# Attention and routed experts on one core: new durations, hand-off times and priorities for the planner that writes the order of the attention stage

## The chip, the cores and the metric

One core of one Trainium2 chip runs the whole program. The metric is device time in microseconds, from the first to the last instruction of one execution, taken as the median of several executions. Lower is better.

## The reference

Two layers follow each other. The first is an attention layer over 8 batches of 8 heads, 1152 keys of 64 numbers, whose queries are averaged in pairs, so that 576 queries are left per head:

```python
q_pool = q.reshape(B, H, S // 2, 2, D).mean(axis=3)
scores = np.matmul(q_pool, k.transpose(0, 1, 3, 2)) / np.sqrt(D)
scores = scores - np.max(scores, axis=-1, keepdims=True)
attn = np.exp(scores)
attn = attn / (np.sum(attn, axis=-1, keepdims=True) + 1e-09)
x = np.matmul(attn, v)
```

The second layer takes the 4608 rows of 512 numbers that come out, gives each row to one of 8 experts of 576 places (greedily, by sorted gate logits), and computes `relu(x @ w1[e]) @ w2[e]` for the rows of each expert. Everything is float32.

## The kernel before

**Attention, pair by pair.** Two heads make a pair; there are 32 pairs, 0 to 31. A pair is handled in 18 steps (9 blocks of 128 keys for each of its two heads). A step has two halves of 288 queries, and each half is two matmuls into one of three PSUM banks `sc` (L466 and L467: the numbers are split into a high and a low part so that the product is exact enough), followed by an exponential on ScalarE (L470). One subtraction per step (L473, on GpSimd in most steps and on VectorE in the others) makes the low part `PM` of the exponentials. For two steps at a time 30 short matmuls (L483, 15 a step) multiply the exponentials with the values; this is called a block of `av` here.

**What a pair needs beforehand.** A bound on the scores of each query has to be known before the first exponential. For that the 27 `mm` matmuls of a pair (L401, into the three PSUM banks `ma`, `mb`, `mc`) compute a coarse product, and VectorE reduces each bank to a maximum (L405). When all 27 are reduced, L422 folds them, a PE transpose (L437) and a VectorE operation (L438) turn them into the tile `AU`, and two tiny transfers (L441) put `AU` into row 64 of `QB`, one of the operands of L467. So the first score matmul of a pair waits for this chain: last `mm`, its reduction, fold, transpose, `AU`, transfer. The `mm` matmuls of a pair run in the middle of the previous pair, and read `BD` (the queries laid out in blocks, L338, made of the averaged queries `QS`, L330, which come from the loaded tile `QD`) and `KH` (the high part of the keys, L347, made from the loaded tile `KD`).

**Transfers.** All of them are issued by SyncE, in one order, on one queue. A pair has loads `QD` (L317), two halves of `KD` (L321) and `VD` (L325), six copies per head inside SBUF that spread the high and low parts over the operands `KA`, `KB`, `QA`, `QB` (L357), the two tiny ones (L441), and every second pair a store (L584). `KA`, `KB`, `QA`, `QB` have two buffers, so the copies of a pair write over those of two pairs earlier, and must wait until the score matmuls of that head are through. An issue that waits holds back all that stand behind it on SyncE.

**The planner.** No order is written by hand. Every operation is added to a list by `Order.add`, with an engine, an assumed duration, the tiles that it reads and writes, and an extra delay `late` until others may use what it writes. `Order.emit` then plays all engines against each other in assumed time: each engine takes, of the operations that are ready, the one with the smallest priority, and the instructions are written in the order in which they were taken. The priority is the nominal place (in steps) plus `LEAD[tag]`; `LATE[tag]` is added to `late`; `WAIT[a][b]` is the assumed time of a hand-off from engine a to engine b and `OWN` the one to an operation of the same engine. A transfer is an operation of engine "SP" with a duration and a `late`. On the chip there is no planner: each engine runs its instructions in the written order, and waits for semaphores.

**Experts.** The second half of the program (`experts`, from about 890 us on) is planned by the same class with its own tables `EOWN`, `EWAIT`, `ELEAD`, `ELATE`.

Of the kernel before, what the change touches and what calls it, by code (L numbers as in the profile page):

```python
# [18 lines left out]
BF = mybir.dt.bfloat16  # L19
# [27 lines left out]
class Order:  # L47
# [3 lines left out]
    OWN = {"PE": 0, "ACT": 190, "DVE": 130, "POOL": 130, "SP": 60}  # L51
    WAIT = {"PE": {"ACT": 260, "DVE": 260, "POOL": 260, "SP": 260},
            "ACT": {"PE": 270, "DVE": 150, "POOL": 180, "SP": 150},
            "DVE": {"PE": 250, "ACT": 150, "POOL": 170, "SP": 150},
            "POOL": {"PE": 170, "ACT": 100, "DVE": 100, "SP": 100},
# [17 lines left out]
    def emit(self):  # L73
# [86 lines left out]
LEAD = {"av0a": 3.8, "av0b": -145.3, "av1a": -3.0, "expa": -95.5, "expb": 46.0, "mm": 1.0, "mc": -122.8, "mr": 77.4,  # L160
        "fold": 194.4, "kl": -40.7, "kh": 79.0, "ql": 264.0, "qs": 149.5, "vl": -310.1, "pmD": -154.7, "pmP": 95.3,
        "gl": -110.7, "x": -28.9, "aug": 20.5, "augt": -216.4, "vabs": -101.5, "store": 99.4, "bd": -11.1, "fill":
        -174.6, "qh": 62.0, "gc": -210.5, "vs": -182.4, "rc": -114.1, "gt": -29.9, "gm": -192.5, "vh": -23.5, "qka":
        3.2, "qkb": 0.4, "gp": -61.0, "gb": 146.7, "augd": 90.5}
LATE = {"mc": 200, "av1b": 0, "pmP": 150, "av0b": 0, "av1a": -350, "pmD": 300, "vh": -100, "av0a": 0, "expa": 50,
        "mm": -50, "mr": -100, "qka": -150, "expb": 50, "qkb": 50, "fold": 250, "aug": -100, "gt": -100, "gc": 0,
        "augt": 400, "gm": 100}
# [66 lines left out]
def attention(ctx, tc, top, kt, qt, v, wg, x_dram, L, npair=NPAIR):  # L234
# [81 lines left out]
    def load(n, t):  # L316
        od.add(t, "SP", 650, lambda: nc.sync.dma_start(QD[0], qt[n]), w=["QD"],  # L317
               late=4000 if not n else 6000 if n > 1 else 13000)
        for z in range(2):
            h = slice(z * M, z * M + M)  # L320
            od.add(t, "SP", 650, lambda h=h: nc.sync.dma_start(KD[0][:, h], kt[n][:, h]), w=[("KD", z)],  # L321
                   late=3000 + 1000 * z if not n else 5500 if n > 1 else 12000)

    def load_v(n, t):
        od.add(t, "SP", 650, lambda: nc.sync.dma_start(VD[0], v[n]), w=["VD"], late=6500)  # L325


    def split(n, t):
        i = n % 2
        od.add(t, "DVE", 650, lock=1, fn=lambda: nc.vector.tensor_tensor(QS[0], QD[0][:, 0], QD[0][:, 1], op=OP.add),  # L330
               r=["QD"], w=["QS"], tag="qs")
        od.add(t + 1, "ACT", 565, lambda: nc.scalar.copy(QH[i], QS[0]), r=["QS"], w=[("QH", i)], tag="qh")
# [7 lines left out]
        for s in range(2):  # L340
            if n:
                od.add(t + 1.1, "ACT", 575, bd(s, nc.scalar.copy), r=["QS"], w=[("BD", i, s)], tag="bd")
            else:
                od.add(t + 0.5, "DVE", 670, bd(s, nc.vector.tensor_copy), r=["QS"], w=[("BD", i, s)], tag="bd")
# [8 lines left out]
    def spread(n, t):  # L353
# [925 lines left out]
```

## Time and profile before

| | |
|---|---|
| median of 3 runs | 1394.06 us (1392.82 to 1394.68) |
| the profiled execution | 1397.87 us, of which the span from first to last instruction is 1396.0 us |
| busy, share of the span | PE 95%, weight loads 84%, VectorE 78%, GpSimd 57%, ScalarE 55% |
| granted TensorE clock | 0.980 of full speed, mean over the span |
| attention, first score matmul to the end | 23.9 to 892.6 us |

The profile numbers the engines' work by line of the kernel. PE is the matmul, PEld the weight load that goes with it, DVE is VectorE, ACT ScalarE, POOL GpSimd, SP SyncE, and a small q (SPq) means the engine's instruction sequencer. In a table of windows each engine has its busy time and, behind an x, the number of its instructions that ran in that window; the columns after the engines are the granted clock, the busy share of the DMA engines and the GB/s that they moved. Since each pair has 36 matmuls of L466, their number in a window tells how many pairs went by. In a list of waits, a row has who waited, for what, then the total, the number and the longest of these waits.

### The profile page before, as it was taken

To read this page: it belongs to the slowest core of one execution; us is meant where nothing else is said; L and a number is where in the kernel's file an instruction comes from. 1 tells how busy PE (TensorE), PEld (TensorE's weight loads), DVE (VectorE), ACT (ScalarE), POOL (GpSimd) and SP (SyncE) were. 2 spreads that over 40 slices of the span, in tenths; PEclk is the share of its full clock that TensorE was granted. 3 is DMA by queue.
4 is the path that set the end of the run, shared out by engine and by line. 5 is a ranking of instruction groups with operands and counts; after the bars stand their busy time and mean duration, and the time that the engine had idled before them with its cause. 6 is when DMAs were issued, how large, how long until landed. Compare 5 with 4: busy or idle time off the path is not lost.

```text
span 1396.0 us, 39631 instructions
## 1 busy us (share of the span) xinstructions
PE 1327.1 (95%) x15415; PEld 1179.3 (84%) x15415; DVE 1083.7 (78%) x2901; ACT 774.7 (55%) x1838; POOL 802.2 (57%) x739
## 2 busy tenths in 40 slices
PE   7899999999998998999999999779999999999996
PEld 6688999998887887998988998658888798898995
DVE  8888999898977889899999996588887678662220
ACT  5576777677665774777767766213424343343330
POOL 4375665655664463665655665335758585676731
PEclk9999999999998999999999999899999999999998
DMA  8866887776875766677767763031354353444400
GB/s 235 210 143 160 198 196 188 192 178 165 192 178 130 193 167 176 154 188 189 191 166 191 167 143 78 19 119 70 138 208 150 112 179 111 134 169 130 147 19 34
DMA packets 86840, 213.23 MB, mean 153 GB/s; under 512 B 12797, under 2 KB 37373, under 8 KB 84477
## 3 DMA queue, kind: packets, MB, share of 16 engines
q1 hardware_dynamic: 78172, 158.26, 46.3%
q0 software_dynamic: 8336, 52.44, 10.7%
q8 instruction: 121, 1.98, 0.6%
q14 instruction: 67, 0.54, 0.1%
q10 hardware_dynamic: 144, 0.02, 0.0%
HBM read 99.63 MB, written 18.87 MB: 85 GB/s over the span
## 4 chain that ended last, share of the span: by engine, by line
PE 78%; DVE 9%; DMA 4%; ACT 3%; issue 3%; SPq 1%; POOL 0%; POOLq 0%; ACTq 0%; DVEq 0%
PE av L483 15%; PE ph L1172 15%; PE po L1202 13%; PE sc L466 11%; PE sc L467 9%; PE ma L401 3%; PE mb L401 3%; PE mc L401 3%; DVE MX L405 3%; ACT P L470 1%; PE rt L845 1%; DVE PM L473 1%; DMA VD<-in_v_dram 1%; DMA QB<-AU 1%; PE po L1199 1%
## 5 line engine op out<-in xcount | busy, mean ns | idle before, releaser
L473 POOL TENSOR_TENSOR PM<-P 128x576 f16<-128x576 f32 x413 | 497.9, 1222 | 374.3 <-ACT P L470 318.3
L470 ACT ACTIVATE P<-sc 128x288 f32<-128x288 f32 x1152 | 420.2, 411 | 224.1 <-PE sc L467 204.8
L466 PE MATMUL sc<-QA,KA 128*128 128x288 f32 x1152 | 364.0, 326 | 11.7 <-ACT P L470 8.2
L467 PE MATMUL sc<-QB,KB 65*128 65x288 f32 (+1 forms) x1152 | 336.5, 301 | 5.4 <-DMA QB<-AU 3.0
L483 PE MATMUL av<-V,P 128*128 128x65 f16 (+1 forms) x5760 | 304.6, 193 | 0.0
L483 PE MATMUL av<-V,PM 128*128 128x65 f16 x2880 | 292.5, 195 | 0.7 <-POOL PM L473 0.7
L483 PEld LDWEIGHTS <-P 128*128 128x128 bf16 x5760 | 271.4, 98 | 24.0 <-issue 1.9
L483 PEld LDWEIGHTS <-PM 128*128 128x128 f16 x2880 | 265.4, 97 | 1.2 <-POOL PM L473 0.9
L466 PEld LDWEIGHTS sc<-QA,KA 128*128 128x128 f32 x1152 | 223.3, 194 | 29.6 <-ACT P L470 21.6
L467 PEld LDWEIGHTS sc<-QB,KB 65*128 65x128 f32 (+1 forms) x1152 | 223.2, 194 | 6.8 <-DMA QB<-AU 3.0
L405 DVE TENSOR_REDUCE MX<-mb 128x1 f32<-128x384 f32 x282 | 154.6, 548 | 24.4 <-PE mb L401 23.7
L405 DVE TENSOR_REDUCE MX<-ma 128x1 f32<-128x384 f32 x282 | 154.3, 547 | 22.5 <-PE ma L401 20.2
L1202 PE MATMUL po<-W2H,HX 128*128 128x512 f32 x512 | 167.4, 402 | 0.0
L405 DVE TENSOR_REDUCE MX<-mc 128x1 f32<-128x384 f32 x281 | 153.9, 548 | 8.1 <-PE mc L401 6.8
L1172 PE MATMUL ph<-XL,W1H 128*128 128x320 f32 (+1 forms) x512 | 152.4, 298 | 1.1 <-DVE XL L1071 1.1
L1172 PE MATMUL ph<-XH,W1H 128*128 128x320 f32 (+1 forms) x512 | 153.1, 299 | 0.0
L1172 PE MATMUL ph<-XH,W1L 128*128 128x320 f32 (+1 forms) x512 | 151.9, 297 | 0.0
L473 DVE TENSOR_TENSOR PM<-P 128x576 f16<-128x576 f32 x163 | 126.4, 796 | 19.4 <-ACT P L470 18.7
L1202 PE MATMUL po<-W2L,HX 128*128 128x512 f32 (+1 forms) x320 | 127.1, 397 | 0.0
L1177 ACT ACTIVATE HX<-ph 128x256 fp32r<-128x256 f32 (+1 forms) x128 | 52.3, 410 | 121.4 <-PE ph L1172 114.1
L401 PE MATMUL ma<-KH,BD 128*128 128x384 f32 x283 | 104.3, 369 | 8.9 <-ACT BD L338 4.6
L1181 DVE SCALAR_TENSOR_TENSOR HX<-ph,HX 128x256 fp32r<-128x256 f32 x128 | 53.4, 420 | 75.8 <-ACT HX L1177 75.6
(238 smaller groups left out, 2315.2 us busy)
## 6 DMA issues: line engine op xcount, KB each, us to landing
QD<-in_qt_dram SPq DMA_DIRECT2D x32, 576.0 KB
KD<-in_kt_dram SPq DMA_DIRECT2D x64, 288.0 KB
VD<-in_v_dram SPq DMA_DIRECT2D x32, 576.0 KB
KA<-KH SPq DMA_DIRECT2D x64, 288.0 KB
KB<-KH SPq DMA_DIRECT2D x64, 288.0 KB
KA<-KL SPq DMA_DIRECT2D x64, 288.0 KB
QA<-QH SPq DMA_DIRECT2D x128, 144.0 KB
QB<-QL SPq DMA_DIRECT2D x64, 144.0 KB
```

Source lines behind the costliest of these rows:

```text
L401: od.add(t, "PE", 180, lambda: nc.tensor.matmul(m[:, :384], BD[i][:, j, :], KH[i][:, 384 * c:384 * c + 384], start=True, stop=True), r=[(" ...
L405: od.add(t, "DVE", 466, lambda: nc.vector.tensor_reduce(MX[i][:, j, c:c + 1], m[:, :384], axis=AX.X, op=OP.max), r=[mk], w=[("MX", i, j, c ...
L466: nc.tensor.matmul(c[:, :288], KA[i][:, s, ks], QA[i][:, s, qs], start=True, stop=False)
L467: nc.tensor.matmul(c[:, :288], KB[i][:kr, s, ks], QB[i][:kr, s, qs], start=False, stop=True)
L470: od.add(g + 0.1 + 0.01 * t, "ACT", 291, lambda c=c, qs=qs: nc.scalar.activation(p[:, qs], c[:, :288], AF.Exp, scale=1.0 / 16), r=[ck], w= ...
L473: od.add(g + 0.2, en, dur, lock=1, fn=lambda: eng.tensor_tensor(pm, p, hi, op=OP.subtract), r=[("P32", g % NP, 0), ("P32", g % NP, 1)], w= ...
L483: nc.tensor.matmul(out, w[:, qs], v, start=kb == 0 and j == 0 and y == 0, stop=kb == NKB - 1 and y == 2, skip_group_check=True)
L845: nc.tensor.matmul(rb[:16 * nb, :8 * nb], GE[:, 8 * z:8 * z + nb], W[:, 8 * z:8 * z + nb], start=z == 0, stop=z == 4, skip_group_check=True)
L1172: nc.tensor.matmul(p, a[:, d, fs], b[:, d, qs], start=z == 0, stop=z == 11)
L1177: nc.scalar.activation(HH[:, f, qs], p, AF.Relu)
L1181: V.scalar_tensor_tensor(HL[:, f, 64 + 256 * hf:320 + 256 * hf], p[:, :256], 0.0, h[:, :256], op0=OP.max, op1=OP.subtract)
L1202: nc.tensor.matmul(o[:n], a[:, z, q0:q0 + n], b[:, z], start=z == 0 and y == 0, stop=z == 7, skip_group_check=True)
```

## The change

The formulas, the tiles and the list of operations are the same: the same 6510 operations are added for the attention stage. What is changed is the numbers that the planner of the attention stage works with. `WAIT` and `OWN` get other hand-off times (for example a result of TensorE counts as usable on VectorE after 205 ns instead of 260). Some fifteen assumed durations on the engines move, most by a few ns; a few by more (the three gate transposes from 327 to 250 ns, the small transposes from 110 to 50). A transfer used to take 650 ns of SyncE and to land a fixed time later (4.0 to 6.5 us for most, more for the first pairs). Now its duration is the time that its bytes take in the queue (2440 ns for the 576 KB of `QD`, 1200 for half of `KD`, 1250 for a copy of 288 KB, 650 for one of 144 KB, 2300 for the store), so that in assumed time transfers follow each other one by one, and it lands 2.0 us after that (2.5 for `VD`). `LEAD` and `LATE` are replaced throughout.

```diff
-    OWN = {"PE": 0, "ACT": 190, "DVE": 130, "POOL": 130, "SP": 60}
-    WAIT = {"PE": {"ACT": 260, "DVE": 260, "POOL": 260, "SP": 260},
-            "ACT": {"PE": 270, "DVE": 150, "POOL": 180, "SP": 150},
+    OWN = {"PE": 0, "ACT": 140, "DVE": 120, "POOL": 130, "SP": 0}
+    WAIT = {"PE": {"ACT": 240, "DVE": 205, "POOL": 220, "SP": 70},
+            "ACT": {"PE": 170, "DVE": 218, "POOL": 225, "SP": 120},
...
-LEAD = {"av0a": 3.8, "av0b": -145.3, "av1a": -3.0, "expa": -95.5, "expb": 46.0, "mm": 1.0, "mc": -122.8, "mr": 77.4,
...
+LEAD = {"aug": 5.86, "augd": 4.23, "augt": -25.48, "av0a": 4.05, "bd": 8.85, "expa": -39.43, "expb": 17.79,
...
     def load(n, t):
-        od.add(t, "SP", 650, lambda: nc.sync.dma_start(QD[0], qt[n]), w=["QD"],
-               late=4000 if not n else 6000 if n > 1 else 13000)
+        od.add(t, "SP", 2440, lambda: nc.sync.dma_start(QD[0], qt[n]), w=["QD"], late=2000)
...
-        od.add(t, "SP", 650, lambda: nc.sync.dma_start(VD[0], v[n]), w=["VD"], late=6500)
+        od.add(t, "SP", 2500, lambda: nc.sync.dma_start(VD[0], v[n]), w=["VD"], late=2500)
...
-            od.add(u, "SP", 650, copy(KA[i], KH[i], 0, s), r=kh, w=[("KA0", i, s)], late=4500)
+            od.add(u, "SP", 1250, copy(KA[i], KH[i], 0, s), r=kh, w=[("KA0", i, s)], late=2000)
...
-        od.add(t, "PE", 180, lambda: nc.tensor.matmul(
+        od.add(t, "PE", 175, lambda: nc.tensor.matmul(
             m[:, :384], BD[i][:, j, :], KH[i][:, 384 * c:384 * c + 384], start=True, stop=True),
```

What it does to the instructions shows in the order on the engines. Three places matter below.

The first is PE where pair 15 begins, that is, just ahead of its first score matmul (`sc` from `QA`, `KA` and `QB`, `KB`); `ma`, `mb`, `mc` are the banks of the coarse products, here those of pair 16. Before:

```order
L401 MATMUL ma<-KH_78,BD_92 128x384
L401 MATMUL mb<-KH_78,BD_92 128x384
L401 MATMUL mc<-KH_78,BD_92 128x384
L401 MATMUL ma<-KH_78,BD_92 128x384
L401 MATMUL mb<-KH_78,BD_92 128x384
L401 MATMUL mc<-KH_78,BD_92 128x384
L401 MATMUL ma<-KH_78,BD_92 128x384
L466 MATMUL sc_144<-QA_89,KA_85 128x288
L467 MATMUL sc_144<-QB_91,KB_87 128x288
L466 MATMUL sc_143<-QA_89,KA_85 128x288
L467 MATMUL sc_143<-QB_91,KB_87 128x288
```

And after the change, at the same first score matmul of pair 15:

```order
L401 MATMUL mc<-KH_78,BD_92 128x384
L466 MATMUL sc_144<-QA_89,KA_85 128x288
L467 MATMUL sc_144<-QB_91,KB_87 128x288
L401 MATMUL ma<-KH_78,BD_92 128x384
L466 MATMUL sc_143<-QA_89,KA_85 128x288
L467 MATMUL sc_143<-QB_91,KB_87 128x288
L401 MATMUL mb<-KH_78,BD_92 128x384
L466 MATMUL sc_145<-QA_89,KA_85 128x288
L467 MATMUL sc_145<-QB_91,KB_87 128x288
L401 MATMUL mc<-KH_78,BD_92 128x384
```

Before, seven coarse products stand in a row (ten of pair 16's, with a block of `av` after the third, stand between the end of pair 14's scores and the start of pair 15's); after, one stands between any two halves. Over the whole stage, leaving out pair 0, the coarse products stood alone 353 times, in twos 118 times, in threes 65 times and in longer rows 9 times; now they stand alone 575 times, in twos 121 times, in threes 5 times and once in a row of five. Between the transpose L437 of pair 15 and its first score matmul there stood two halves, two blocks of `av` and ten coarse products before; now there stand ten halves, three blocks and nine coarse products. What stands there differed from pair to pair before; after the change two nearly equal patterns alternate from pair 5 to pair 30 (the even pairs have twelve halves).

The second place is SyncE around the tiny transfers of `AU` for pair 15. Before:

```order
L357 DMA QB_91<-QL_83 64x576 x2
L357 DMA KA_84<-KH_78 64x1152
L357 DMA KA_84<-KL_80 64x1152
L357 DMA KB_86<-KH_78 64x1152
L317 DMA QD_106<-in_qt_dram 128x1152
L441 DMA QB_91<-AU 1x9x64
L357 DMA QA_88<-QH_81 64x576 x4
L441 DMA QB_91<-AU 1x9x64
L321 DMA KD_105<-in_kt_dram 128x576 x2
```

After:

```order
L357 DMA KA_84<-KH_78 64x1152
L357 DMA KA_84<-KL_80 64x1152
L357 DMA KB_86<-KH_78 64x1152
L357 DMA QA_88<-QH_81 64x576 x2
L325 DMA VD_107<-in_v_dram 128x1152
L441 DMA QB_91<-AU 1x9x64 x2
L357 DMA QB_90<-QL_83 64x576
L318 DMA QD_106<-in_qt_dram 128x1152
L357 DMA KA_84<-KH_78 64x1152
```

Before, the copies into the second head's half of `KA_84`, `KB_86` (which must wait for the last steps of pair 14) and the load of `QD` stand ahead of the first tiny transfer, and four copies between the two; after, both tiny transfers stand together, with the copies of pair 16's first head and the load of `VD` ahead of them, and the second head's copies behind. On VectorE, the addition that makes `QS` (L330) for pair 16 stood right behind `AU` of pair 15 and right ahead of the first reduction for pair 16; now what stands beside `AU` of pair 15 is the addition for pair 17, a whole pair earlier.

The third place is the beginning of SyncE's list, where the operands of pair 0 (`KA_84`, `KB_86`, `QA_88`, `QB_90`) and the loads for pair 1 stand. Before:

```order
L325 DMA VD_107<-in_v_dram 128x1152
L321 DMA KD_105<-in_kt_dram 128x576
L357 DMA KA_84<-KH_78 64x1152
L357 DMA KB_86<-KH_78 64x1152
L357 DMA KA_84<-KH_78 64x1152
L357 DMA KB_86<-KH_78 64x1152
L357 DMA KA_84<-KL_80 64x1152 x2
L317 DMA QD_106<-in_qt_dram 128x1152
L357 DMA QA_88<-QH_81 64x576 x2
L357 DMA QB_90<-QL_83 64x576
L357 DMA QA_88<-QH_81 64x576 x2
L357 DMA QB_90<-QL_83 64x576
```

After:

```order
L325 DMA VD_107<-in_v_dram 128x1152
L357 DMA KA_84<-KH_78 64x1152
L357 DMA KB_86<-KH_78 64x1152
L357 DMA KA_84<-KL_80 64x1152
L357 DMA KA_84<-KH_78 64x1152
L357 DMA KA_84<-KL_80 64x1152
L357 DMA QA_88<-QH_81 64x576 x2
L357 DMA QB_90<-QL_83 64x576
L357 DMA KB_86<-KH_78 64x1152
L357 DMA QA_88<-QH_81 64x576 x2
L357 DMA QB_90<-QL_83 64x576
L318 DMA QD_106<-in_qt_dram 128x1152
```

Before, half of pair 1's `KD` stood ahead of all copies and pair 1's `QD` in the middle of them; after, all twelve copies of pair 0 come first, and pair 1's `QD` and `KD` follow. On VectorE the addition that reads this `QD` (L330 of pair 1) stands, before and after, ahead of the two operations that write the bound of pair 0 into `QB` (L432); after the change it also stands ahead of the fold (L422) of pair 0.

More of the change, by code (lines that the diff above doesn't have):

```diff
@@ L316, in load @@
     def load(n, t):
[L317 to L318 removed]
+        od.add(t, "SP", 2440, lambda: nc.sync.dma_start(QD[0], qt[n]), w=["QD"], late=2000)
         for z in range(2):
             h = slice(z * M, z * M + M)
[L321 to L322 removed]
+            od.add(t, "SP", 1200, lambda h=h: nc.sync.dma_start(KD[0][:, h], kt[n][:, h]), w=[("KD", z)],
+                   late=2000)
     def load_v(n, t):
[L325 removed]
+        od.add(t, "SP", 2500, lambda: nc.sync.dma_start(VD[0], v[n]), w=["VD"], late=2500)
     def split(n, t):
         i = n % 2
[L330 removed]
+        od.add(t, "DVE", 666, lock=1, fn=lambda: nc.vector.tensor_tensor(QS[0], QD[0][:, 0], QD[0][:, 1], op=OP.add),
                r=["QD"], w=["QS"], tag="qs")
[L332 removed]
+        od.add(t + 1, "ACT", 580, lambda: nc.scalar.copy(QH[i], QS[0]), r=["QS"], w=[("QH", i)], tag="qh")
         e2, eng2, d2 = ("DVE", nc.vector, 665) if n > AT["sp"] else ("POOL", nc.gpsimd, 1110)
@@ L341, in split @@
             if n:
-                od.add(t + 1.1, "ACT", 575, bd(s, nc.scalar.copy), r=["QS"], w=[("BD", i, s)], tag="bd")
+                od.add(t + 1.1, "ACT", 565, bd(s, nc.scalar.copy), r=["QS"], w=[("BD", i, s)], tag="bd")
             else:
@@ L374, in values @@
                r=["VD"] + ([("MS", NB - 1)] if not n else []), w=[("VM", i)], tag="vabs")
-        od.add(t + AT["vs"] - 1, "PE", 60, lambda: nc.tensor.matmul(mb[:, :1], ones, VM[i].bitcast(BF)[:, 1:2], start=True, stop=True),
+        od.add(t + AT["vs"] - 1, "PE", 30, lambda: nc.tensor.matmul(mb[:, :1], ones, VM[i].bitcast(BF)[:, 1:2], start=True, stop=True),
                r=[("VM", i)], w=["mb"], tag="vs")
@@ L469, in step @@
             od.add(g + 0.01 * t, "PE", 266, qk, r=qr, w=[ck], tag="qk" + "ab"[t])
-            od.add(g + 0.1 + 0.01 * t, "ACT", 291, lambda c=c, qs=qs: nc.scalar.activation(
+            od.add(g + 0.1 + 0.01 * t, "ACT", 293, lambda c=c, qs=qs: nc.scalar.activation(
                 p[:, qs], c[:, :288], AF.Exp, scale=1.0 / 16), r=[ck], w=[("P32", g % NP, t)], tag="exp" + "ab"[t])
-        en, eng, dur = ("DVE", nc.vector, 655) if g % NSTEP in pd or (n == npair - 1 and g % 3 == 2 and kb > 5) else ("POOL", nc.gpsimd, 1110)
+        en, eng, dur = ("DVE", nc.vector, 666) if g % NSTEP in pd or (n == npair - 1 and g % 3 == 2 and kb > 5) else ("POOL", nc.gpsimd, 1110)
         od.add(g + 0.2, en, dur, lock=1, fn=lambda: eng.tensor_tensor(pm, p, hi, op=OP.subtract),
@@ L524, in tr @@
                 nc.tensor.transpose(m[:, 128 * z:128 * z + 128], X[u][:, 3 * q + z], ident)
-        od.add(t, "PE", 327, tr, r=xk, w=[mk], tag="gt")
-        od.add(t, "ACT", 371, lambda: nc.scalar.copy(XT[q].rearrange("p c t -> p (c t)"), m[:, :384]),
+        od.add(t, "PE", 250, tr, r=xk, w=[mk], tag="gt")
+        od.add(t, "ACT", 362, lambda: nc.scalar.copy(XT[q].rearrange("p c t -> p (c t)"), m[:, :384]),
                r=[mk], w=[("XT", q)], tag="gc")
@@ L583, in store @@
         bp, c, u = n // H, n % H // 2, n // 2 % NX
-        od.add(t, "SP", 650, lambda: nc.sync.dma_start(
+        od.add(t, "SP", 2300, lambda: nc.sync.dma_start(
             x_dram[bp * 2 * M:(bp + 1) * 2 * M].rearrange("(j p) d -> p j d", p=128)[:, :, 128 * c:128 * c + 128], X[u]),
-            r=[("X", u, z, s) for z in range(2) for s in range(2)], w=[("xd", n)], late=4000, tag="store")
+            r=[("X", u, z, s) for z in range(2) for s in range(2)], w=[("xd", n)], late=2000, tag="store")
     od.cur = None
```

40 lines of the change are left out of this document (17 added, 23 removed), and 7 rows, old and new, of tables (LATE, LEAD).

## Prediction

> **What bounds the kernel now.** The page comes first, for the engine that sets the end.
>
> ```profile
> PE 1327.1 (95%) x15415; PEld 1179.3 (84%) x15415; DVE 1083.7 (78%) x2901; ACT 774.7 (55%) x1838; POOL 802.2 (57%) x739
> PE 78%; DVE 9%; DMA 4%; ACT 3%; issue 3%; SPq 1%; POOL 0%; POOLq 0%; ACTq 0%; DVEq 0%
> ```
>
> PE carries 78% of the chain that ended last; 9% of it runs over VectorE and 4% over transfers, and that is where an order can win. The change touches the attention stage alone, so windows of that stage come next: all engines, then the matmuls of L466 alone.
>
> ```profile
> core 0: us, PE busy (x) PEld busy (x) DVE busy (x) ACT busy (x) POOL busy (x), PEclk, DMA share, GB/s
> 23.90:121.70 97.80, 88.03 (x1142) 77.75 (x1143) 86.29 (x192) 61.89 (x148) 49.90 (x48) 0.92 0.72 182
> 121.70:867.00 745.30, 721.40 (x10599) 661.40 (x10598) 665.99 (x1404) 525.07 (x1293) 436.04 (x364) 0.99 0.71 173
> 144.40:321.80 177.40, 175.77 (x2659) 162.99 (x2654) 163.00 (x349) 132.24 (x324) 109.01 (x91) 1.00 0.78 192
> ...
> 23.90:121.70 97.80, 35.62 (x108) 22.59 (x109) 0.92 0.72 182
> 121.70:867.00 745.30, 316.86 (x1008) 193.92 (x1009) 0.99 0.71 173
> 144.40:321.80 177.40, 78.74 (x252) 47.88 (x252) 1.00 0.78 192
> ```
>
> At 36 matmuls of L466 a pair, pairs 0 to 2 took 97.80 / 3 = 32.6 us each, pairs 3 to 30 took 745.30 / 28 = 26.62 us each, and inside those, pairs 4 to 10 took 177.40 / 7 = 25.34 us each. So the old order already holds 25.34 over seven pairs, at full clock with PE busy 99%, and loses 1.28 us a pair on average against that. Where it loses shows in the waits of PE's weight loads, first of pairs 3 to 30, then of pairs 4 to 10.
>
> ```profile
> PEld sc L466 <- ACT P L470: 17.4, 40, 1.2
> PEld ma L401 <- DVE MX L405: 10.0, 20, 1.0
> PEld mb L401 <- DVE MX L405: 8.6, 16, 1.7
> PEld ma L401 <- ACT BD L338: 4.9, 7, 1.5
> PEld mc L401 <- DVE MX L405: 3.4, 12, 0.7
> PEld sc L467 <- DMA QB<-AU: 3.0, 1, 3.0
> ...
> PEld sc L466 <- ACT P L470: 3.7, 8, 1.2
> PEld ma L401 <- DVE MX L405: 0.6, 1, 0.6
> PEld mb L401 <- DVE MX L405: 0.4, 1, 0.4
> PEld mc L401 <- DVE MX L405: 0.3, 1, 0.3
> ```
>
> Waits for a bank that VectorE has still to reduce are 22.0 us over 28 pairs, but 1.3 over the seven good ones; waits for `BD` and for the tiny `AU` transfer do not occur in the good ones at all. One bad place, the start of pair 15, read in the chain and in SyncE's timeline:
>
> ```profile
> 427.45 0.27 DVE AU L438
> 427.72 0.68 DVE QS L330
> 428.42 0.67 ACT BD L338
> 429.10 0.68 ACT BD L338
> 429.82 0.45 PE ma L401
> 430.30 1.49 DVE MX L405 x3
> 432.31 5.81 DMA QB<-AU
> 438.17 0.61 PE sc L467
> ...
> 430.91 1.35 SPq L317 DMA_DIRECT2D QD<-in_qt_dram  x1
> 432.31 1.46 SPq L441 DMA_DIRECT2D QB<-AU  x1
> ```
>
> Three faults of the order meet here. `AU` is ready at 427.72, but its transfer is issued at 432.31, behind the copies and the load of `QD` that stand ahead of it on SyncE. On PE ten coarse products stand ahead of the scores; the first waits for `BD`, which waits for `QS`, and the others for VectorE, one reduction each. And with so little else between the transpose and the scores, nothing hides the 5.81 us.
>
> **The change part by part.** No instruction is added or removed; the sum is made of waits.
>
> *Distance to the AU transfer.* What PE has to do between a pair's transpose and its first score matmul covers the chain over `AU`. Its price from a stretch without waits:
>
> ```profile
> 189.72 0.18 PE mb L401
> 189.90 0.13 PE sc L466
> 190.03 0.13 PE sc L467
> 190.16 0.94 PE av L483 x30
> ```
>
> So a half costs 0.26 us, a block of `av` 0.94, a coarse product 0.18. Pair 15 had 2 x 0.26 + 2 x 0.94 + 10 x 0.18 = 4.2 us of cover; now it has 10 x 0.26 + 3 x 0.94 + 9 x 0.18 = 7.0, and every pair from 5 to 30 has 7.0 or about 7.6. The chain itself, from the rows above, is at least 0.27 for `AU` and 5.81 for a transfer that met a full queue: 6.1, so it is covered with 0.9 to spare. The 3.0 us go.
>
> *Coarse products one by one.* A row of three or more fills the three banks faster than VectorE empties them (1.49 us for three reductions against 0.54 us of matmuls). Such rows fall from 74 to 6, so I take the waits for VectorE down to the rate of the good stretch: 22.0 - 4 x 1.3 = 16.8 us. The waits for `BD` (4.9) go, as `QS`, which `BD` is made of, is added up a whole pair ahead of its coarse products now. Waits for an exponential fall to the good rate, 17.4 - 4 x 3.7 = 2.6 us.
>
> *The clock.* The stretches with the bad starts ran below full clock:
>
> ```profile
> 435.20:556.10 120.90, 110.92 (x1526) 99.02 (x1526) 104.16 (x216) 76.28 (x186) 62.01 (x52) 0.95 0.67 170
> 556.10:682.30 126.20, 124.22 (x1821) 116.08 (x1821) 113.86 (x237) 93.92 (x231) 75.93 (x64) 0.98 0.71 175
> ```
>
> 0.05 x 120.90 + 0.02 x 126.20 = 8.5 us of full-speed work were lost; without the gaps that set it off, as in the good stretch at 1.00, they come back. The Trainium skill ("TensorE: Matmul & The Clock Gate", Part 1) says that the clock halves after an idle window of about 3.4 us. This case's longest single wait here is 3.0 us, below that, and the clock fell all the same. Taken by the rule alone, an order whose waits stay under 3.4 us would keep the whole 8.5 us; by the rows, shorter waits close together can cost some of it.
>
> Sum of waits for pairs 3 to 30: 3.0 + 16.8 + 4.9 + 2.6 + 8.5 = 35.8 us. The paces say the same in another way: 28 x (26.62 - 25.34) = 35.8. They are two views of one thing, and their agreeing says that little else was lost. From below, nothing need be gained, and a wait that comes back in each pair could cost (rivals). From above, PE's own work is 72 matmuls of 0.13, 9 blocks of 0.94 and 27 products of 0.18: 22.7 us a pair, so 28 x (26.62 - 22.7) = 110 us is out of any order's reach. I take 35.8, since the good stretch carries the same instructions.
>
> *The first pair.* Here the new order looks worse. VectorE's timeline, then SyncE's:
>
> ```profile
> 20.30 0.18 DVE L422 TENSOR_REDUCE CM<-MX 128x9 f32<-128x27 f32 x1
> 22.72 0.76 DVE L330 TENSOR_TENSOR QS<-QD 128x576 f32<-128x576 f32 x1 [2.24 <-DMA QD<-in_qt_dram]
> 23.51 1.43 DVE L432 SCALAR_TENSOR_TENSOR QB<-mb,ndiag 9x576 fp32r<-9x576 f32 x2
> ...
> 14.56 0.62 SPq L317 DMA_DIRECT2D QD<-in_qt_dram  x1
> 19.68 0.60 SPq L357 DMA_DIRECT2D QB<-QL  x1
> ```
>
> VectorE waited 2.24 us for pair 1's `QD`, issued at 14.56, and the bound of pair 0 (L432) stood behind it. Now this load stands behind the last copy of pair 0, issued at 19.68 before; half of `KD` no longer stands ahead of the copies, which should bring that forward by one or two us. If `QD` takes the 22.72 - 14.56 = 8.2 us to land again, `QS` starts about 3 us later. The fold, too, now waits behind it (0.18 and the transpose), but a shorter queue ahead may win as much. I take +3 us, between 0 (all hidden by the lighter queue) and +6 (the full 5.1 us and the fold).
>
> *Pairs 0 to 2 and 31.* The first three cost 32.6 us each, 7.3 above the good pace, at clock 0.92. The new order has shorter rows of coarse products there, but less cover for `AU` (2.5 to 4.3 us of PE work). The last pair has no coarse products left. I take 0, between -8 and +8.
>
> Total: 1396.0 - 35.8 + 3 = 1363.2 us of span. The profiled execution took 1397.87, 1.9 above its span and 3.8 above the median of the runs, so against the median: 1394.06 - 32.8 = 1361 us.
>
> **The rivals.** *Tighter still.* Even the good stretch has room: weight loads and VectorE are busy 162.99 and 163.00 of 177.40 us, 92% or 23.3 us a pair. A pace halfway, 24.3, gives 28 x (26.62 - 24.3) = 65 us: 1394 - 65 + 3 = 1332. For it speak the regular spacing; against it, two engines at 96% with waits on each other. The Trainium skill ("Trainium Kernel Development and Optimization", Performance Expectations) calls matmul busy time a bad measure of closeness to the limit and weight-load busy time a good one. The 99% of PE beside the 92% of weight loads agrees, and that is the room this rival would use.
>
> *Part of the gain.* The good stretch also has the highest DMA share, 0.78 against 0.71. If the queue cannot hold that through 28 pairs, or VectorE at 92% has no slack for a late tile, pairs take about 26.0: 28 x 0.62 = 17 us, 1394 - 17 + 3 = 1380.
>
> *A wait in every pair: slower.* The new order repeats itself, so one misjudged hand-off returns 26 times. The place would be the `AU` chain again: both tiny transfers stand right behind the 576 KB of `VD`, and on VectorE `AU` stands behind work that follows the fold. With 7.0 us of cover, an `AU` delayed by 2 us plus the 5.81 us transfer and 0.27 exceeds it by 1.1; with the clock falling as it did at pair 15 the stop is worth double. At 25.34 + 2.2 = 27.5 us a pair the time is 28 x 0.9 + 3 = 28 us longer: 1422. It decides from 1.2 us a pair on (1.28 less 3/28). Against it: the transfer of 5.81 was the bad case, with its issue behind four others.
>
> *No change.* If VectorE's own work set the pace, a new order of it would be worth nothing. Its 665.99 / 28 = 23.8 us a pair against 26.62 speak against that.
>
> **How the numbers follow.** The forecast, 1361, has 0.52, its own range 1350 to 1372; tighter 0.14; part of the gain 0.20; a wait in every pair 0.09; no change 0.05, of which 0.04 lie within 0.2% (2.8 us, about what a measurement of this kernel can tell from none) and 0.01 above. Faster: 0.52 + 0.14 + 0.20 = 0.86; same 0.04; slower 0.10. The range 1336 to 1388 leaves out the lower half of the tighter case, the slow side and a little of the partial one, about 0.2.
>
> **What would show it.** Right: pairs 3 to 30 at 25 to 25.7 us by the count of L466; clock 1.00 from pair 3 on; waits of weight loads for `MX` under 8 us in those 28 pairs, and none for `BD` or `QB<-AU`; the first score matmul near 27 us. Wrong: the same wait at the same place in pair after pair, most of all for `QB<-AU` at L467; a clock of 0.9 in many windows; or a first score matmul at or before 24 us.

## The result and the profile after

The changed kernel takes 1341.84 us (median of 4 runs, 1339.0 to 1343.25) against 1394.2 for the kernel before: a ratio of 0.9623, 95% interval 0.9606 to 0.9641. The profiled execution took 1342.09 us with a span of 1340.3, so 55.7 us of span are gone (1396.0 before). The page's busy row and its chain of waits now read:

```profile
PE 1296.5 (97%) x15415; PEld 1169.3 (87%) x15415; DVE 1060.4 (79%) x2901; ACT 788.9 (59%) x1838; POOL 775.6 (58%) x739
PE 86%; DVE 6%; DMA 3%; issue 2%; ACT 1%; POOL 0%; SPq 0%; POOLq 0%; DVEq 0%; ACTq 0%
```

PE carries 86% of the chain, 78% before. The work of PE is the same 15415 matmuls, so what went is waiting and half clock. The windows, in the columns of the prediction's windows, tell where. The first three rows are all engines, the last is the matmuls of L466 alone:

```profile
25.80:111.70 85.90, 80.63 (x1106) 73.08 (x1106) 80.85 (x188) 63.84 (x150) 44.01 (x47) 0.96 0.77 196
111.70:811.30 699.60, 697.16 (x10605) 655.21 (x10604) 648.56 (x1409) 538.18 (x1292) 414.68 (x365) 1.00 0.76 186
386.00:511.40 125.40, 125.40 (x1903) 117.64 (x1902) 117.54 (x256) 98.53 (x237) 73.39 (x65) 1.00 0.80 198
...
111.70:811.30 699.60, 315.40 (x1008) 191.70 (x1008) 1.00 0.76 186
```

Pairs 3 to 30 (1008 matmuls of L466) take 699.60 us instead of 745.30, or 24.99 a pair instead of 26.62: 45.7 us less. Pairs 0 to 2, counted from the first score matmul, take 85.90 instead of 97.80: 11.9 less. The first score matmul is 1.9 us later (25.8 against 23.9). 1.9 - 11.9 - 45.7 = -55.7, so the last pair and the experts together give nothing. The third row is pairs 14 to 18, the worst five of the kernel before:

```profile
400.60:556.10 155.50, 141.73 (x1952) 125.75 (x1949) 132.45 (x278) 98.79 (x239) 78.82 (x67) 0.96 0.69 172
```

These five hold 155.50 - 125.40 = 30.1 of the 45.7 us. PE is now shown as busy through all of them (125.40 of 125.40).

The waits of PE's weight loads in pairs 3 to 30, to be laid beside the first six rows of that view in the prediction:

```profile
PEld mb L401 <- DVE MX L405: 8.5, 14, 0.6
PEld sc L466 <- ACT P L470: 3.6, 7, 1.1
...
PEld mc L401 <- DVE MX L405: 0.3, 1, 0.3
```

Waits for VectorE's reductions fell from 22.0 to 8.8 us, waits for exponentials from 17.4 to 3.6; `BD` (4.9) and the tiny `AU` transfer (3.0) are gone from the list. (In the list of PE's own waits one stop of 0.7 us for `AU` is left, at the start of pair 12.) The start of pair 15, first VectorE's, then SyncE's timeline:

```profile
405.19 0.27 DVE L438 TENSOR_SCALAR AU<-mb 9x128 fp32r<-9x128 f32 x1
...
405.49 1.57 SPq L441 DMA_DIRECT2D QB<-AU  x2
```

`AU` starts at 405.19 and its transfers are issued at 405.49, at once, 6.2 us ahead of the pair's first score matmul at 411.7. Before, the transfer was issued 4.6 us after `AU` was ready (427.72 to 432.31).

### The profile page after: what moved, and what is told of

It reads as the page before. It is cut to its first block, busy times and chain, and to the rows that moved or that the text cites. A ratio compares the mean times of both kernels' runs of the same rounds, so it can differ in the third digit from the quotient of the medians.

```text
span 1340.3 us, 39670 instructions
## 1 busy us (share of the span) xinstructions
PE 1296.5 (97%) x15415; PEld 1169.3 (87%) x15415; DVE 1060.4 (79%) x2901; ACT 788.9 (59%) x1838; POOL 775.6 (58%) x739
## 4 chain that ended last, share of the span: by engine, by line
PE 86%; DVE 6%; DMA 3%; issue 2%; ACT 1%; POOL 0%; SPq 0%; POOLq 0%; DVEq 0%; ACTq 0%
PE av L483 18%; PE ph L1172 16%; PE po L1202 14%; PE sc L466 12%; PE sc L467 10%; PE mb L401 4%; PE mc L401 4%; PE ma L401 3%; DVE MX L405 2%; DMA KD<-in_kt_dram 2%; PE rt L845 1%; PE av L524 1%; PE po L1199 1%; PE av L536 1%; DMA KA<-KH 1%
## 5 line engine op out<-in xcount | busy, mean ns | idle before, releaser
L473 POOL TENSOR_TENSOR PM<-P 128x576 f16<-128x576 f32 x413 | 471.6, 1158 | 345.2 <-ACT P L470 328.1
L470 ACT ACTIVATE P<-sc 128x288 f32<-128x288 f32 x1152 | 433.9, 410 | 161.4 <-PE sc L467 128.1
L466 PE MATMUL sc<-QA,KA 128*128 128x288 f32 x1152 | 361.8, 321 | 2.3 <-ACT P L470 2.1
L467 PE MATMUL sc<-QB,KB 65*128 65x288 f32 (+1 forms) x1152 | 336.4, 298 | 3.1 <-issue 1.7
L466 PEld LDWEIGHTS sc<-QA,KA 128*128 128x128 f32 x1152 | 220.4, 191 | 10.0 <-ACT P L470 6.7
L467 PEld LDWEIGHTS sc<-QB,KB 65*128 65x128 f32 (+1 forms) x1152 | 219.5, 191 | 3.9 <-issue 2.8
L473 DVE TENSOR_TENSOR PM<-P 128x576 f16<-128x576 f32 x163 | 118.4, 748 | 12.4 <-ACT P L470 12.3
L1202 PEld LDWEIGHTS po<-W2H,HX 128*128 128x128 f32 x512 | 94.3, 189 | 17.1
```

Of the source, the lines that this page charges most:

```text
L466: nc.tensor.matmul(c[:, :288], KA[i][:, s, ks], QA[i][:, s, qs], start=True, stop=False)
L467: nc.tensor.matmul(c[:, :288], KB[i][:kr, s, ks], QB[i][:kr, s, qs], start=False, stop=True)
L470: od.add(g + 0.1 + 0.01 * t, "ACT", 293, lambda c=c, qs=qs: nc.scalar.activation(p[:, qs], c[:, :288], AF.Exp, scale=1.0 / 16), r=[ck], w= ...
L473: od.add(g + 0.2, en, dur, lock=1, fn=lambda: eng.tensor_tensor(pm, p, hi, op=OP.subtract), r=[("P32", g % NP, 0), ("P32", g % NP, 1)], w= ...
L1202: nc.tensor.matmul(o[:n], a[:, z, q0:q0 + n], b[:, z], start=z == 0 and y == 0, stop=z == 7, skip_group_check=True)
```

## The experiments

Where one engine's list was edited, the planner first made its order as usual; then that list alone was rearranged, the lists of the other engines kept their own order, and the instructions were written so that nothing stands ahead of what it depends on. Added lines shift the line numbers in some experiments. "The pace" is the mean of pairs 3 to 30, counted by the score matmuls as above.

### Priorities alone, numbers of the model alone

The change has two halves: the tables `LEAD` and `LATE`, and the planner's durations, hand-offs and landings. Each was put alone into the kernel before. The first:

```diff
-LEAD = {"av0a": 3.8, "av0b": -145.3, "av1a": -3.0, "expa": -95.5, "expb": 46.0, "mm": 1.0, "mc": -122.8, "mr": 77.4,
...
+LEAD = {"aug": 5.86, "augd": 4.23, "augt": -25.48, "av0a": 4.05, "bd": 8.85, "expa": -39.43, "expb": 17.79,
...
```

> The new LEAD and LATE with the old hand-off times, durations and transfer model. Counted on PE's order, the cover of the AU transfer is 6.5 us or more from pair 4 on (7.5 to 8.9 in most pairs) and only 9 rows of three or more coarse products are left. Theory A (time follows from the cover and from the spacing of the coarse products, whatever numbers made the order): pairs 3 to 30 near 25.2 us, 1340 to 1362 us. Theory B (what counts is that transfers are planned as a queue, so that loads and copies are issued when the queue has room): most of the gain is lost, 1375 us or more, with waits for KD, KA or QB copies in many pairs.

Measured: 1349.03 us, ratio 0.9665 (0.9646 to 0.9683), pace 25.12, in theory A's range. So the priorities alone bring 3.35% of the 3.77%. The two largest waits of its weight loads in pairs 3 to 30 are

```profile
PEld sc L467 <- ACT P L471: 10.4, 21, 1.1
PEld sc L467 <- ACT BD L339: 7.1, 11, 0.6
```

The second half is the changed kernel with the old `LEAD` and `LATE`:

> The new hand-off times, durations and transfer model with the old LEAD and LATE. PE's order has 64 rows of three or more coarse products and a cover of only 2.5 to 3.3 us for the AU transfer in pairs 5 to 29. Theory A: PE waits 1.5 to 2.5 us for QB<-AU in most pairs, pairs 3 to 30 at 26.3 to 27.5 us, 1380 to 1415 us. Theory B (the transfer model carries the gain): 1365 us or less.

Measured: 1457.14 us, ratio 1.0445 (1.0423 to 1.0468), pace 28.53, slower than both theories had it. The two largest waits of PE in pairs 3 to 30:

```profile
PE ma L400 <- ACT BD L337: 24.6, 15, 1.8
PE sc L466 <- DMA QB<-QL: 20.3, 12, 3.1
```

The new numbers with the old priorities are worse than the old pair of both. Nor does the loss sit where it was expected: not at the `AU` transfer, but at `BD` and at the copies of the low part of the queries, which come late.

The third part of the model was tried on its own: the changed kernel with the transfers' old durations and landings.

```diff
-        od.add(t, "SP", 2440, lambda: nc.sync.dma_start(QD[0], qt[n]), w=["QD"], late=2000)
+        od.add(t, "SP", 650, lambda: nc.sync.dma_start(QD[0], qt[n]), w=["QD"],
+               late=4000 if not n else 6000 if n > 1 else 13000)
...
```

> The changed kernel with the old durations and landing times of the transfers alone (650 ns of SyncE and 4.0 to 6.5 us). PE's order has 17 rows of three or more coarse products, and a cover of 7.0 us or more in 24 of 27 pairs from 5 on, with 4.5 and 5.3 in two. Theory A: pairs 3 to 30 near 25.3 us, 1345 to 1362 us. Theory B: 1370 us or more, with waits for transfers that the old model thinks have landed.

Measured: 1372.06 us, ratio 0.9832 (0.9812 to 0.9852), pace 25.72. The time is in theory B's range, but not for theory B's reason: in pairs 3 to 30 the weight loads wait 13.4 us for exponentials and 6.0 + 4.9 + 1.4 = 12.3 us for reductions, and no wait for a transfer is in the list. With all of the old model the new priorities gave 1349, with the new engine times and the old transfers 1372, with all of the new model 1342. The parts do not add up: each model makes another order of the same priorities.

### The first pairs

The changed kernel with the load of `QD` for pair 1 moved forward on SyncE, behind the first copy into `KB` of pair 0:

```diff
+def qd_early(l, info):
+    qd = next(i for i in l if info(i)[1] == 1 and info(i)[2] == "QD")
+    l = [i for i in l if i != qd]
+    at = next(k for k, i in enumerate(l) if info(i)[1] == 0 and info(i)[2][0] == "KB")
+    return l[:at + 1] + [qd] + l[at + 1:]
```

> The changed kernel with one load moved: pair 1's QD is issued right after the first two copies of pair 0 instead of behind all twelve, into 3 us in which SyncE only waits for the low part of the keys. VectorE waits 2.99 us for this load ahead of the bound of pair 0. Theory C (the first pair is held by this load): the first score matmul comes at 22.5 to 23.5 us instead of 25.8, and the time is 2 to 3 us shorter. Theory D (the first pairs are held by VectorE's own work and by the preparation of pairs 1 and 2): the first score matmul is as early, but the first matmul of pair 3 stays at 111 to 112 us and the time within 0.7 us.

Measured: 1340.72 us, ratio 0.9609 (0.959 to 0.9628): no difference that can be told from the changed kernel's 0.9623. Its window of pairs 0 to 2:

```profile
23.11:111.80 88.69, 81.00 (x1110) 73.01 (x1107) 81.00 (x188) 64.47 (x150) 44.07 (x47) 0.96 0.77 196
```

The first score matmul comes 2.7 us earlier, at 23.11, and pair 3 begins where it did (111.80 against 111.70). VectorE is busy 81.00 us in these pairs, as in the changed kernel (80.85): the earlier start is given back already in pair 0 (pair 1 starts at 56.3 us against 56.0). That fits the theory that their preparation on VectorE holds them; the run shows only that the start does not.

### Undoing single faults in the old order

The faults that the prediction named were taken out of the kernel before, one list at a time. First PE's: on PE the coarse products that stood in rows were put one by one behind the following halves or blocks (rows of three and more: from 74 to 4), with the other lists as they were.

```diff
+def spread_mm(l, info):
+    out, held, row = [], [], 0
...
+        if tag == "mm" and n:
+            if row >= 2 or held:
+                held.append(i)
...
+        elif tag in ("qka", "qkb", "av0a"):
+            out.append(i)
+            row = 0
+            if held:
+                out.append(held.pop(0))
+                row = 1
```

> The order before the change with PE's coarse products alone moved apart: the third and later ones of a row are put one by one behind the next halves or blocks. Rows of three or more fall from 74 to 4; nothing else moves. Theory A (the prediction's: such rows fill the three banks, and the 22.0 us of waits for VectorE come from them): those waits fall below 8 us and the time to 1366 to 1382 us. Theory E (rows of three stand in the good stretch too, 15 of them in pairs 4 to 10 with 1.3 us of waits; PE waits for VectorE where VectorE is late for another reason): the time stays within 6 us of 1394, and the waits move to the scores or stay.

Measured: 1429.93 us, ratio 1.024 (1.0209 to 1.0271), pace 27.53: slower, which neither theory had. The waits of weight loads, then of VectorE, in pairs 3 to 30:

```profile
PEld sc L512 <- ACT P L516: 18.9, 33, 2.8
PEld sc L513 <- DMA QB<-AU: 12.5, 2, 6.6
PEld mb L447 <- DVE MX L451: 10.7, 17, 1.7
PEld ma L447 <- DVE MX L451: 8.9, 17, 1.5
PEld mc L447 <- DVE MX L451: 2.4, 7, 0.9
...
DVE MX L451 <- PE mb L447: 34.3, 38, 5.7
```

With the rows gone, weight loads wait for the reductions 10.7 + 8.9 + 2.4 = 22.0 us, as long as before, and for exponentials 18.9 (17.4 before). VectorE, whose list still had the reductions early, now waited up to 5.7 us for a product that PE had put later, and the `AU` chain behind it came late (12.5 us at two pair starts).

Next SyncE's: the tiny `AU` transfers put ahead of the next pair's copies and `QD`, and then both edits together.

```diff
+def au_first(l, info):
...
+            if n2 != n and n2 is not None and t2 != "augd" and (w2 == "QD" or w2[0] in ("QA0", "QA1")
+                    or w2[0] in ("KA0", "KA1", "KB", "QB0") and w2[2] == 1):
+                l[j - 1], l[j] = l[j], l[j - 1]
+                j -= 1
```

> The order before the change with SyncE's list alone changed: the two AU transfers of a pair are issued ahead of the next pair's copies for the second head, its Q copies and the QD load that stood before them. Theory A: AU lands up to 4.6 us earlier at pair 15 and 8.6 at pair 19, the half clock there goes, 1383 to 1390 us. Theory E (at the bad starts the tiles made ahead of the coarse products are late as well, so PE waits there anyway): 1391 to 1396 us.

> Both edits of the two runs before on the order before the change. Theory A: 1358 to 1375 us, about what the change itself brings. Theory E: 1385 us or more, since a late tile on VectorE or ScalarE is neither.

Measured: the transfers alone 1394.62 us, ratio 0.9994 (0.9979 to 1.0009), no gain that can be told from none; both 1411.19 us, ratio 1.012 (1.0095 to 1.0145), pace 27.04. Both times lie in theory E's ranges. With the transfers alone, pairs 14 and 18 still take 34.4 and 36.6 us (34.6 and 36.5 before). But pair 15, whose first matmul of L467 had waited for `AU`, takes 27.0 instead of 28.8, and its pairs 3 to 30 together

```profile
123.86:864.99 741.13, 719.15 (x10599) 660.78 (x10598) 665.41 (x1404) 524.76 (x1293) 435.82 (x364) 0.99 0.71 175
```

are 745.3 - 741.1 = 4.2 us shorter in this one profile, while pair 3 starts 2.1 us later (123.86 against 121.73). The moved transfers took away the wait for `AU`; what makes pairs 14 and 18 long is something else. Where the edit of PE's list had made it the late one, an earlier transfer gave back 1.2% of the 2.4%.

### Rows of three in the new order

The opposite edit: in the changed kernel, for pairs 5 to 30, the coarse products were gathered in threes on PE (rows of three or more: from 6 to 124).

```diff
+def in_threes(l, info):
...
+        if tag == "mm" and n and 5 <= n <= 30:
+            held.append(i)
+            if len(held) == 3:
+                out += held
+                held = []
```

> The changed kernel with PE's coarse products gathered: of pairs 5 to 30 they are held back past halves until three stand together, though not past a block of av. Rows of three or more rise from 6 to 124, and nothing else moves. Theory A: PE waits for VectorE in them, 1.5 us of reductions against 0.5 us of matmuls, 0.4 us or more a row and 45 us or more in all: 1385 us or more. Theory E: VectorE keeps up and the rows cost little, 1342 to 1352 us.

Measured: 1384.77 us, ratio 0.9921 (0.9893 to 0.9948), pace 26.49. 28 x (26.49 - 24.99) = 42 us are lost at full clock; the time is at the lower edge of theory A's (1385 us or more). The waits of weight loads in pairs 3 to 30:

```profile
PEld sc L507 <- ACT P L511: 24.9, 53, 1.0
PEld mb L442 <- DVE MX L446: 14.7, 55, 0.3
PEld ma L442 <- DVE MX L446: 8.2, 33, 0.3
PEld mc L442 <- DVE MX L446: 3.6, 13, 0.3
```

Waits for reductions are 14.7 + 8.2 + 3.6 = 26.5 us, and waits for exponentials rose from 3.6 to 24.9. To tell which of the two VectorE's time makes, the same order was run with reductions that leave out half of the coarse product:

```diff
-        od.add(t, "DVE", 464, lambda: nc.vector.tensor_reduce(MX[i][:, j, c:c + 1], m[:, :384], axis=AX.X, op=OP.max),
+        od.add(t, "DVE", 464, lambda: nc.vector.tensor_reduce(MX[i][:, j, c:c + 1], m[:, :192], axis=AX.X, op=OP.max),
```

> The changed kernel with its coarse products gathered in rows of three on PE (the experiment that took 1385), and with the reductions of L405 cut to 192 of 384 columns, so that half of the coarse product is left out of the bound. Theory F says the 43 us that the rows of three cost are VectorE's time to empty three banks: with reductions about half as long most of it goes, 1335 to 1355. If the rows cost through something else on PE (more switching between shapes, exponentials that come late because the scores do), they cost as much as with full reductions: 1370 to 1390.

Measured: 1358.33 us, ratio 0.971 (0.9693 to 0.9726), pace 25.58. The two largest waits of weight loads:

```profile
PEld sc L507 <- ACT P L511: 25.4, 55, 1.1
PEld L524 <- issue: 18.4, 116, 0.2
```

Not one wait for a reduction is left, and 28 x (26.49 - 25.58) = 25.5 us come back, which is close to the 26.5 of those waits. The other 28 x (25.58 - 24.99) = 16.5 us stay, with the exponentials waited for as long as before (25.4) and many short stops at the `av` blocks for which the profile has no releaser (18.4, where the changed kernel has 2.2 and the rows of three with full reductions 12.4). ScalarE's own waits for a score (`ACT P <- PE sc`), 106.7 us in pairs 3 to 30 of the changed kernel, are 169.1 with the rows of three and 135.1 with the shorter reductions. So a row of three costs twice in this order: the banks are emptied too slowly, and the scores behind the row come late for ScalarE.

### Is VectorE the bound?

The same shorter reductions, which leave out half of the coarse product, in the two kernels themselves, with their orders unchanged.

> The kernel before in its own order, but each of VectorE's reductions for the bound (L405) reads only 192 of the 384 columns of its bank, so half of the coarse product is left out of the bound; nothing else is changed. In the kernel before these reductions took 0.548 us each, 27 in a pair, so some 4 to 7 us of VectorE work fall away in each pair. Theory F (what is lost before is lost between two lists that do not fit: a row of coarse products fills the three banks faster than VectorE empties them, and VectorE is late for the rest) expects that a faster VectorE forgives most of the bad order: pairs 3 to 30 at 24.5 to 25.5 us, waits of weight loads for MX under 8 us, time 1340 to 1365. Theory G (the loss of the old order is in the transfers and the half clock and the waits for VectorE only follow from it) expects less than a third of the way: 1380 to 1395.

> The changed kernel in its own order, with the same cut: each reduction of L405 reads 192 of 384 columns, half of the coarse product is left out of the bound. If the changed kernel is bound by PE's own list (theory F: waits of only some 0.8 us a pair are left), little can come back: 1325 to 1342, at most 0.6 us a pair in 28 pairs. If VectorE at 94% still sets the pace through the hand-offs (theory H), a pair falls below 24.2 us and the time below 1322.

Measured, kernel before with half the columns: 1381.35 us, ratio 0.9887 (0.9864 to 0.991), pace 26.01. The reductions, by groups of instructions, took 0.351 us where they took 0.548, and VectorE's busy time in pairs 3 to 30 fell from 665.99 to 548.81 us:

```profile
L405 DVE TENSOR_REDUCE MX<-mb 128x1 f32<-128x384 f32 x282 | 154.6, 548 | 24.4 <-PE mb L401 23.7
...
L405 DVE TENSOR_REDUCE MX<-mb 128x1 f32<-128x192 f32 x282 | 99.0, 351 | 62.0 <-PE mb L401 59.1
...
118.53:846.86 728.33, 710.97 (x10599) 657.88 (x10598) 548.81 (x1402) 523.65 (x1293) 431.68 (x364) 0.99 0.72 178
```

Here theory F falls in its strong form: 117 us less work for VectorE gained 745.3 - 728.3 = 17.0 us, and the time is in theory G's range. Waits for reductions halved (22.0 to 10.9), and most of the rest of the old order's loss, with 4.6 us for `BD`, stayed where it was:

```profile
PEld sc L466 <- ACT P L470: 15.8, 38, 1.1
PEld ma L401 <- DVE MX L405: 6.3, 13, 0.8
PEld sc L467 <- DMA QB<-AU: 4.9, 2, 4.4
PEld mb L401 <- DVE MX L405: 4.1, 6, 1.5
```

Changed kernel with half the columns: 1340.74 us, ratio 0.9582 (0.9563 to 0.9602); the median is 1.1 us below the changed kernel's 1341.84. By the ratios, each to the kernel before run beside it (0.9582 against 0.9623), the gain is 0.4%; by the medians it is 0.1%. Its window and its largest wait:

```profile
111.90:808.03 696.13, 693.98 (x10605) 653.24 (x10605) 527.65 (x1408) 538.45 (x1292) 415.20 (x365) 1.00 0.76 187
...
PEld mb L401 <- DVE MX L405: 8.4, 13, 0.6
```

VectorE has 648.56 - 527.65 = 121 us less to do, and the 28 pairs are 699.60 - 696.13 = 3.5 us shorter (24.86 a pair instead of 24.99). Faster VectorE work is worth little in the new order: VectorE is not its bound. The one wait for a bank that is left did not shrink with the reductions (8.4 against 8.5), so what sets it is not how long a reduction takes; where the reduction stands is what is left, which no run tried.

### A wait in every pair

The rival that would have made the kernel slower: in the changed kernel, for pairs 5 to 30, the two tiny `AU` transfers were put behind the copies of the next pair's second head, which must wait for the last steps of the pair before.

```diff
+def au_last(l, info):
+    l = list(l)
+    for n in range(5, 31):
+        au = [i for i in l if info(i)[0] == "augd" and info(i)[1] == n]
+        rest = [i for i in l if i not in au]
+        last = max(k for k, i in enumerate(rest) if info(i)[1] == n + 1 and info(i)[2][0] in ("KA0", "KA1", "KB")
+                   and info(i)[2][2] == 1)
...
```

> The changed kernel, with SyncE's list alone changed: for pairs 5 to 30 the two tiny transfers of AU stand behind the copies of the next pair's second head into KA and KB, which have to wait until the last score matmuls of the pair before are through. This is the wait in every pair that was held to be a rival of the forecast. If the transfer's place on SyncE carries the pair starts, the tiny transfers are issued about when the pair begins and land 2 us or more later: each of 26 pairs loses 2 to 6 us, 1395 to 1500, with waits of L467 for QB<-AU in pair after pair. If the first matmuls of L466 and the work that stands between them cover it anyway, the time stays within 1340 to 1355.

Measured: 1543.82 us, ratio 1.1033 (1.1014 to 1.1053), pace 32.12. The window of pairs 3 to 30 and the waits of PE in it:

```profile
111.40:1010.70 899.30, 757.01 (x10605) 707.57 (x10605) 657.65 (x1409) 539.92 (x1292) 415.23 (x365) 0.91 0.59 145
...
PE sc L503 <- DMA QB<-AU: 97.0, 19, 6.7
PE sc L503 <- issue: 44.0, 7, 6.6
```

The 28 pairs lose 899.30 - 699.60 = 199.7 us, 7.7 for each of the 26 moved pairs. The waits at L503, one for each moved pair (19 + 7), are 97.0 + 44.0 us, 5.4 a pair; for the 44.0 the profile names no releaser, but they stand at the same place. The rest fits the half clock: at 0.91 over 899.30 us, 81 us of full-speed work are lost, 3.1 a pair, part of it while PE waits anyway.

## Why the prediction was right, and where it was off

**Pairs 3 to 30: forecast -35.8, measured -45.7 us.** By the prediction's own terms:

| term | forecast | measured | from |
|---|---|---|---|
| `AU` transfer | 3.0 | 3.0 | 3.0 to none |
| waits for reductions | 16.8 | 13.2 | 22.0 to 8.8 |
| `BD` | 4.9 | 4.9 | 4.9 to none |
| exponentials | 2.6 | 13.8 | 17.4 to 3.6 |
| half clock | 8.5 | 8.5 | granted clock 1.00 |
| sum | 35.8 | 43.4 | of 45.7; 2.3 not accounted for |

The term that was mis-sized is the last of the waits: "Waits for an exponential fall to the good rate". Pairs 4 to 10 of the old order were taken as what an order can reach, with 3.7 us of these waits in seven pairs. The new order has 3.6 in 28. The agreement of the two sums (35.8 twice) was no check on this, because both views took the same seven pairs for their goal. The rows-of-three experiment shows one thing that makes the exponentials late, and the prediction had put it under the reductions only: products in a row push the scores back (24.9 us of these waits in place of 3.6). It is not the whole: in the kernel before, with the rows spread, these waits were 18.9 us against 17.4. What else brings them down to 3.6 is open.

**The reductions.** The size is near (16.8 forecast, 13.2 measured), and that rows make such waits is shown by the rows-of-three run. But "rows of three fall from 74 to 6, so the waits go" was not enough of a reason. With the rows spread and nothing else moved, the old kernel waited the same 22.0 us and was slower. The rows seem to matter only inside lists that fit each other, such as the new ones, where gathering them cost 42 us. That the fit as a whole does it, rather than one more single fault not tried, is what the failed single edits suggest; which of the moves in the new lists are needed is open.

**`AU`.** Cover against the chain fits what came: the wait at pair 15 is gone. Its place on SyncE, one of the "three faults", is enough to take that wait away: moved alone it shortened pairs 3 to 30 by 4.2 us in its profile, against the 3.0 of this term. In the whole time that gain does not show (0.9994).

**The first pair: forecast +3, measured +1.9 us.** Most of the mechanism came as described; VectorE's timeline after:

```profile
24.54 0.76 DVE L330 TENSOR_TENSOR QS<-QD 128x576 f32<-128x576 f32 x1 [2.99 <-DMA QD<-in_qt_dram]
25.21 0.17 DVE L422 TENSOR_REDUCE CM<-MX 128x9 f32<-128x27 f32 x1
25.88 1.43 DVE L432 SCALAR_TENSOR_TENSOR QB<-mb,ndiag 9x576 fp32r<-9x576 f32 x2 [0.49 <-PE mb L430]
```

VectorE waited 2.99 us for `QD` (2.24 before), and the fold and the bound came behind it. The start that this is compared with was not held by that chain alone: before, the profile names the copy `QB<-QL` as what released the first score matmul at 23.9 us. And putting the load on the path to the end was wrong: when it was moved forward the 2.7 us did not reach pair 3.

**Pairs 0 to 2: forecast 0 within 8 either way, measured -11.9.** Outside its bounds. The prediction weighed the shorter cover for `AU` against the shorter rows, took nothing for both, and did not price the waits that stood there. The waits of weight loads in these pairs, the largest before and then after:

```profile
PEld sc L466 <- ACT P L470: 3.8, 6, 1.6
PEld sc L466 <- DMA QB<-QL: 3.2, 1, 3.2
PEld mb L401 <- DVE MX L405: 2.9, 4, 1.3
PEld sc L467 <- DMA QA<-QH: 2.2, 1, 2.2
PEld ma L401 <- DVE MX L405: 2.2, 5, 0.9
PEld mc L401 <- DVE MX L405: 1.5, 4, 0.6
PEld ma L401 <- ACT BD L338: 1.4, 1, 1.4
```

```profile
PEld sc L467 <- issue: 2.8, 2, 2.0
PEld sc L466 <- ACT P L470: 2.0, 5, 0.6
...
PEld mc L401 <- DVE MX L405: 1.2, 3, 0.6
PEld ma L401 <- DVE MX L405: 0.8, 3, 0.4
PEld mb L401 <- DVE MX L405: 0.8, 2, 0.5
```

Waits for reductions fell from 6.6 to 2.8 us, those for exponentials from 3.8 to 2.0, the 1.4 for `BD` are gone, and the clock rose from 0.92 to 0.96: 0.08 x 97.80 - 0.04 x 85.90 = 4.4 us of full-speed work. Together that is 3.8 + 1.8 + 1.4 + 4.4 = 11.4 of the 11.9, by the same terms as in the later pairs. The copies of the queries give nothing here: the 3.2 us for `QB<-QL` ended at 23.9, where the count of these pairs begins, and the 2.2 for `QA<-QH`, at the start of pair 1, have in their place a stop of 2.0 us without a named releaser.

**Total and rivals.** The medians differ by 52.4 us, where 32.8 were forecast. 1341.84 lies in the stated range of 1336 to 1388, but outside the forecast's own, 1350 to 1372. By pace (24.99) the kernel is nearer to the forecast (25.34) than to "tighter still" (24.3); by time it is nearer to that rival (1332 us), and what makes the difference are the 11.9 us of the first pairs, which both had put at nothing. Of the signs of being right, the clock of 1.00 and the missing waits for `BD` and `QB<-AU` came; the pace is just under the 25 to 25.7 named, the waits for `MX` are 8.8 us where under 8 were named, and the first score matmul is at 25.8 where 27 was. "Tighter still" saw room because weight loads were busy 92% of the good stretch while PE was at 99%. In the new order weight loads are at 655.21 / 699.60 = 94%, PE at 99.7%, and taking 121 us off VectorE frees 3.5. That points to PE's own list as the bound; no run shortened that list, so it is not shown. The Trainium skill ("Trainium Kernel Development and Optimization", Performance Expectations) prefers weight-load busy time as the measure of closeness; by it 6% of room is left, which no run here reached. The floor of 22.7 us a pair in the prediction left out the small transposes and the gate, whose matmuls (L536) stand in even pairs: from pair 5 on, odd pairs now take 24.0 to 24.2 us and even ones 25.5 to 26.0 in most, 27.0 at most. "A wait in every pair" was a real mechanism, priced too low: 7.7 us a pair against 2.2, once the transfer's issue comes after the end of the pair before. In the new order the issue comes 6.2 us ahead of the first score matmul at pair 15, and the transfer has that time to land. "Part of the gain" fails on its reason: the queue holds a share of 0.76 over the 28 pairs.

## What to carry to other kernels

Before a new order is priced from a good stretch of the old one, ask of each kind of wait whether the good stretch is its floor, or just a place where the old order happens to be better. A planner's numbers and its priorities belong together: here the new priorities gave 0.9665 with the old numbers, the old priorities 1.0445 with the new numbers, and a single list of the old order moved by hand made the kernel slower or left its time as it was. Whether an engine sets the pace is shown at small cost by shortening its work with the order unchanged: 121 us off VectorE were worth 3.5 us in the new order, and 117 us only 17 in the old.

## What the hardware showed

The granted clock fell after shorter waits than the 3.0 us that the prediction set beside pair 15. At that pair the clock was at 0.50 already from 434.80 to 435.20 us, ahead of the wait for `AU` (PE stood still from 435.6 to 438.2); what lay before were waits of PE of 1.4, 0.3 and 0.7 us. In the kernel with the model's numbers alone, PE waited 1.8 us for `BD` between 409 and 413.2 us (the only wait of PE in that window), and the 3.2 us from 413.2 ran at half clock. But the same wait of 1.8 us, ending at 468.6, was followed by full clock:

```profile
PE ma L400 <- ACT BD L337: 1.8, 1, 1.8
...
413.20:416.40 3.20, 3.20 (x13) 3.20 (x13) 2.68 (x6) 1.64 (x4) 1.43 (x2) 0.50 0.99 233
...
468.60:473.00 4.40, 4.36 (x26) 4.00 (x26) 3.93 (x9) 3.70 (x9) 2.92 (x3) 1.00 1.01 226
```

Of the twelve waits of 1.6 to 1.8 us of PE in pairs 3 to 30 of that run, six were followed by half clock within 4 us and six were not. What decides between them no run here tells.

The Trainium skill ("TensorE: Matmul & The Clock Gate", Part 1) puts the idle window before the clock halves at about 3.4 us. These rows do not agree: waits of half that length were followed by a fall, though not always. So a wait on PE can cost more than its own length even when it is short, here 1.8 us of waiting and some 1.6 us of lost speed.

Smaller reductions are not proportionally shorter: 192 columns instead of 384 took 0.351 instead of 0.548 us.
